# Four unrolled batches of a fallback path folded into two nested loops

## Chip, cores and metric

The kernel runs on one core of one Trainium2 chip. The metric is the time of one execution in microseconds (us), as a median of several runs. Work is spread over the core's engines: TensorE (PE, with its weight loads shown as PEld), VectorE (DVE), ScalarE (ACT), GpSimd (POOL), and SyncE (SP), which in this kernel issues most transfers. Each engine has a sequencer of its own that runs that engine's instruction stream in order. An instruction of the sequencer alone (a wait, a branch, a register load, the issue of a transfer) is written with a q: PEq, SPq.

## What is computed

```python
# q [4, 12288, 128], kv [4, 384, 32, 128], w_sr [128, 128]
kv_pool = kv.reshape(B, H // r, r, W // r, r, C).mean(axis=(2, 4))      # r = 4
k = v = kv_pool.reshape(B, -1, C) @ w_sr                                # 768 rows a batch
a = softmax(q @ k.T / sqrt(C));  x = (a @ v).reshape(B * 12288, C)
logits = x @ w_gate                                                     # 8 experts, the best 2
out = x + sum over the two experts of w * ((x @ A[e]) @ B[e])           # A: 128 to 16, B: 16 to 128
```

Spatial pooling and a projection give 768 keys a batch, which are the values as well; 49152 query rows attend to them, and each resulting row goes through the best two of eight rank-16 adapters.

## The kernel before, in words

The kernel has two paths in one program.

The **main path** (lines 51 to 605) does all of the work on ordinary data. It takes the 49152 rows in 96 chunks of 512. For each chunk it makes scores (L249) and their exponentials (L250), the weighted sum of the values (`weigh`, L260), normalises (L267, L271), transposes (L317), and runs the adapters (`down` L340, `apply_gate` L345, `up` L361, `give` L367 to L371, which also issues the transfer of the result). The order of all instructions is written out by hand (`manual_schedule`), with batch b+1's keys and values prepared while batch b is worked on. It works in 16-bit types and without the subtraction of the maximum, so it also counts, in `count_ok`, `values_ok`, `tail_ok` and `all_ok`, whether all sums and values lie in a safe range. The result is one integer, `bad`, written at L422.

The last two chunks are given out by ScalarE's queue (L603, L605, `give(..., queue=nc.scalar)`); all earlier results go through SP's queue.

The **general path** (lines 610 to 695) stands behind `tc.If(bad_v != 0)`. Every engine loads `bad` into a register (L607) and branches on it (L610). Where `bad` is zero, an engine jumps over the whole general path to a short block that stands behind it in its instruction stream. In that block each engine waits for its own last work and brings the semaphores to the values that the general path would have left; SP waits there for the transfers whose semaphores the general path uses, one semaphore after another (these waits carry the line of the If, L610). Then comes an end block, in which SP waits once more for every semaphore of the kernel, and all engines meet at a barrier twice (these carry the line of the call, L721).

Before the change the general path is, for each of four batches, written out four times: keys (L620 to L624) and values (L625 to L631) in float32 from the pooled rows `kpT[b]` in SBUF, then a hardware loop over 128 rows at a time (`tc.For_i`, L632) with a body of 20-odd operations.

Of the kernel before, what the change touches and what calls it, by code (L numbers as in the profile page):

```python
# [10 lines left out]
FP32 = mybir.dt.float32  # L11
# [10 lines left out]
def kernel(  # L22
# [10 lines left out]
    nc = tc.nc  # L33
    P = 128
    B, N, C = q.tensor.shape
# [3 lines left out]
    NKV = (H // 4) * (W // 4)  # L39
# [12 lines left out]
    kvpool = ctx.enter_context(tc.tile_pool(name="kvpool", bufs=4))  # L52
# [12 lines left out]
    qdram = ctx.enter_context(tc.tile_pool(name="qdram", bufs=1, space=bass.MemoryType.DRAM))  # L65

    def mtile(shape, dtype=FP32, name="hd"):
        return ps_h.tile(shape, dtype, tag="hd", name=name)

    mm = nc.tensor.matmul  # L70
# [7 lines left out]
    kvt = {}  # L78
# [38 lines left out]
    w_sr_sb = const.tile([P, P], FP32)  # L117
# [3 lines left out]
    wext = const.tile([P, C + E], FP32)  # L121
# [11 lines left out]
    kpT, kfT, vext = {}, {}, {}  # L133
# [363 lines left out]
    for c in range(1, NCH - 1):  # L497
        b, k = divmod(c, CPB)
# [11 lines left out]
        if cs < NCH and cs % GRP == 0:  # L510
            g = cs // GRP
# [98 lines left out]
    with tc.If(bad_v != 0):  # L610
# [5 lines left out]
        big2 = kvpool.tile([P, 4 * 1024], FP32, tag="kvt", name="g_e")  # L616
        e = big2[:, 0:NKV]
        eT = big2[:, 1024:1024 + NKV].rearrange("p (j t) -> p j t", j=NJ)
        for b in range(B):
            for h in range(2):  # L620
                s = slice(h * NKV // 2, (h + 1) * NKV // 2)
                k_ps = mtile([P, NKV // 2], name="gk_ps")
                mm(k_ps, w_sr_sb, kpT[b][:, s], start=True, stop=True)
                nc.vector.tensor_copy(k32[:, s], k_ps)  # L624
            for h in range(2):  # L625
                v_ps = mtile([P, NJ // 2, C + E], name="gv_ps")
                for g in range(NJ // 2):
                    j = h * NJ // 2 + g
                    mm(v_ps[:, g], kpT[b][:, j * P:(j + 1) * P], wext,
                       start=(g == 0), stop=(g == NJ // 2 - 1))  # L630
                nc.vector.tensor_copy(v32[:, h * NJ // 2:(h + 1) * NJ // 2], v_ps)  # L631
            with tc.For_i(b * N, (b + 1) * N, P) as t0:  # L632
                qt = run.tile([P, C], FP32, tag="g_q", name="g_q", bufs=1)
                nc.sync.dma_start(qt, qflat[bass.ds(t0, P), :])
                q_ps = mtile([P, P], name="gq_ps")
# [4 lines left out]
                for h in range(2):  # L640
                    mm(s_ps[:, h, 0:NKV // 2], qTf, k32[:, h * NKV // 2:(h + 1) * NKV // 2],
                       start=True, stop=True)
# [9 lines left out]
                for h in range(2):  # L652
                    e_ps = mtile([P, NJ // 2, P], name="ge_ps")
                    for g in range(NJ // 2):
                        j = h * NJ // 2 + g
                        mm(e_ps[:, g], e[:, j * P:(j + 1) * P], id_f32, is_transpose=True,
                           start=(g == 0), stop=(g == NJ // 2 - 1))
# [68 lines left out]
```

## Time and profile before

| what | us |
|---|---|
| median of 3 runs | 410.38 (409.85 to 410.66) |
| the profiled execution's own time | 410.03 |
| its span, from the first to the last instruction | 408.2 |
| around the span | 1.8 |
| PE busy | 385.4 (94% of the span) |
| DVE busy | 346.5 (85%) |
| ACT busy | 298.2 (73%) |
| POOL busy | 164.6 (40%) |

The granted TensorE clock is 0.993 on average. A row of the profile names the line, the engine, the operation, the tiles as out<-in, and the count. The queues of transfers are listed with packets, megabytes and the share of time; the kind `instruction` is the fetching of instructions from memory by the engines' sequencers.

### The profile page before, as it was taken

The page shows a single profiled execution, that of the slowest core. Times are in us where ns is not written, and L with a number is a line of the kernel's source. Part 1 is how long each engine was busy: PE and PEld are TensorE (multiplying, and loading weights), DVE is VectorE, ACT ScalarE, POOL GpSimd, SP SyncE. Part 2 cuts the span into 40 slices and gives each one's busy share as a digit, 9 for nine tenths or more (in the row PEclk, how much of TensorE's full clock was granted, in tenths as well). Part 3 has the DMA queues.
Part 4 walks back from the last instruction along what each step waited for, and adds up shares of the span by engine and source line. Part 5 has one row for each costly group of instructions (what it writes and reads, how often), then busy time and mean ns, then how long its engine had stood idle before and what let it go on. Part 6 is the DMA issues. An engine that isn't in the chain of part 4 may idle for free.

```text
span 408.2 us, 11562 instructions
## 1 busy us (share of the span) xinstructions
PE 385.4 (94%) x4607; PEld 306.0 (75%) x4607; DVE 346.5 (85%) x972; ACT 298.2 (73%) x357; POOL 164.6 (40%) x314
## 2 busy tenths in 40 slices
PE   4888999999999999999999999999999999999992
PEld 1446777887878787887878787777878788787792
DVE  3765799898899899898899899898899989899982
ACT  1648887886778877886678877876777888877751
POOL 1011489782113487882113487892212212122120
PEclk9999999999999999999999999999999999999997
DMA  8979899979467999979378999798185474221113
GB/s 256 404 234 174 260 292 231 303 164 156 117 119 127 327 244 284 318 175 157 92 143 133 323 219 296 241 260 161 54 181 117 142 159 130 79 79 68 66 75 140
DMA packets 69789, 76.52 MB, mean 187 GB/s; under 512 B 49664, under 2 KB 49920, under 8 KB 69376
## 3 DMA queue, kind: packets, MB, share of 16 engines
q1 hardware_dynamic: 67264, 63.45, 55.6%
q0 software_dynamic: 704, 11.54, 16.5%
q10 hardware_dynamic: 1760, 0.73, 0.7%
q8 instruction: 38, 0.62, 0.6%
q14 instruction: 23, 0.19, 0.1%
HBM read 50.53 MB, written 36.70 MB: 214 GB/s over the span
## 4 chain that ended last, share of the span: by engine, by line
PE 82%; DVE 10%; ACT 2%; issue 2%; DMA 2%; SPq 0%; DVEq 0%
PE xps L260 32%; PE sg L249 27%; PE t_ps L317 9%; PE d_ps L361 5%; PE h_ps L340 4%; DVE xn L271 2%; DVE hg L345 2%; DMA kvt<-in_kv_dram 2%; ACT tt L250 1%; PE v_ps L174 1%; DVE top L278 1%; PE k_ps L167 1%; DVE vmax L207 1%; DVE osb L369 1%; DVE xh L326 1%
## 5 line engine op out<-in xcount | busy, mean ns | idle before, releaser
L250 ACT ACTIVATE tt<-sg 128x1024 f16<-128x1024 f32 x288 | 282.8, 1022 | 76.7 <-PE sg L249 75.7
L249 PE MATMUL sg<-qT,kfT 128*128 128x512 bf16 x576 | 170.8, 379 | 1.5 <-ACT tt L250 0.7
L260 PE MATMUL xps<-vext,tt 128*128 128x137 f16 x2304 | 170.8, 224 | 0.5 <-DVE xn L271 0.4
L260 PEld LDWEIGHTS <-tt 128*128 128x128 f16 x2304 | 154.0, 112 | 23.1 <-DVE xn L271 1.5
L369 DVE TENSOR_TENSOR osb<-d_ps,xn 128x512 f32<-128x512 f32 x90 | 62.1, 690 | 17.3 <-PE d_ps L361 13.9
L271 DVE TENSOR_TENSOR xn<-xps,rinv_all 128x548 f32<-128x548 f32 x96 | 69.9, 729 | 3.3
L284 POOL TENSOR_TENSOR m<-top 128x8 f32<-128x8 f32 x47 | 10.9, 232 | 152.1 <-DVE top L278 151.9
L143 POOL TENSOR_TENSOR kvt<-kvt 128x1024 f32<-128x1024 f32 x27 | 64.0, 2370 | 3.9 <-DMA kvt<-in_kv_dram 1.5
L345 DVE TENSOR_TENSOR hg<-h_ps,gw 128x512 bf16<-128x512 f32 x94 | 63.8, 679 | 0.6 <-PE h_ps L340 0.4
L326 DVE COPY xh<-t_ps 128x1024 bf16<-128x1024 bf16 (+1 forms) x93 | 62.5, 672 | 0.0
L361 PEld LDWEIGHTS <-xh 128*128 128x128 bf16 x384 | 29.2, 98 | 26.1 <-issue 6.1
L249 PEld LDWEIGHTS <-kfT 128*128 128x128 bf16 x576 | 45.2, 98 | 3.7 <-issue 1.7
L340 PEld LDWEIGHTS <-xh 128*128 128x128 bf16 x384 | 29.2, 98 | 20.9 <-issue 0.7
L278 DVE MAX8 top<-xn 128x8 f32<-128x8 f32 x384 | 36.0, 156 | 3.3
L361 PE MATMUL d_ps<-b_bf,xh 128*128 128x128 bf16 x360 | 34.8, 219 | 3.3 <-DVE hg L345 3.0
L340 PE MATMUL h_ps<-a_bf,xh 128*128 128x128 bf16 x376 | 36.3, 219 | 0.6 <-DVE cnt L409 0.6
L317 PE MATMUL t_ps<-id_bf,xn 128*128 128x128 bf16 x376 | 36.3, 219 | 0.0
L317 PE MATMUL t_ps<-id_bf,hg 128*128 128x128 bf16 x376 | 36.3, 219 | 0.0
L299 POOL TENSOR_SCALAR th<-th 128x64 f32<-128x64 f32 x47 | 17.4, 370 | 37.4 <-ACT th L297 37.4
L317 PEld LDWEIGHTS <-xn 128*128 128x128 bf16 x384 | 26.0, 98 | 0.0
L317 PEld LDWEIGHTS <-hg 128*128 128x128 bf16 x384 | 25.4, 98 | 0.1
L267 DVE RECIPROCAL rinv_all<-xps 128x4 f32<-128x4 f32 x96 | 17.6, 183 | 8.2 <-PE xps L260 5.2
(103 smaller groups left out, 220.1 us busy)
## 6 DMA issues: line engine op xcount, KB each, us to landing
kvt<-in_kv_dram SPq DMA_DIRECT2D x48, 512.0 KB, 7.2
out_dram<-osb SPq DMA_DIRECT2D x94, 256.0 KB, 3.1
q_bf<-in_q_dram POOLq DMA_DIRECT2D x22, 512.0 KB, 6.6
q<-in_q_dram SPq DMA_DIRECT2D x2, 1024.0 KB, 10.1
out_dram<-osb ACTq DMA_DIRECT2D x2, 256.0 KB, 3.4
qT<-q_bf SPq DMA_TRANSPOSE x22, 7.1
w_in<-in_w_sr_dram ACTq DMA_DIRECT2D x1, 64.0 KB, 1.9
a_f<-in_moe_A_dram ACTq DMA_DIRECT2D x1, 64.0 KB, 10.1
```

Of the source, the lines that this page charges most:

```text
L143: eng.tensor_tensor(v[:, 0], v[:, 0], v[:, d], op=ALU.add)
L249: mm(sg[:, k], kfT[b][:, j * P:(j + 1) * P], qc, start=True, stop=True)
L250: nc.scalar.activation(tt[c][:, 2 * r:2 * r + 2], sg, AF.Exp, bias=0.0, scale=scale)
L260: mm(o, tt[c][:, j, rows], vext[b][:, j], start=(j == 0 and s % 2 == 0), stop=(j == NJ - 1 and s % 2 == 1), skip_group_check=True)
L271: nc.vector.tensor_tensor(xn[c].rearrange("p (b s) v -> p b s v", b=2), xv, ri.rearrange("p (b s) -> p b s", b=2).unsqueeze(3).broadcast_t ...
L278: nc.vector.max(gin[c // 2][:, (c % 2) * NS + s], xn[c][:, s, C:C + E])
L317: mm(t_ps[:, k, s], src, id_bf, is_transpose=True, start=(i == 0), stop=(i == len(todo) - 1), skip_group_check=True)
L326: nc.vector.tensor_copy(xh[:, lo:hi_], t_ps[:, lo:hi_])
L340: mm(hps[c][:, s], xT[c][:, s], a_bf, start=(s == 0), stop=(s == NS - 1))
L345: nc.vector.tensor_tensor(hg[c].rearrange("p s (e r) -> p (s e) r", r=RK), hps[c].rearrange("p s (e r) -> p (s e) r", r=RK), g.rearrange(" ...
L361: mm(dps[c][:, s], hgT[c][:, s], b_bf, start=(s == 0 and not plus_x), stop=(s == NS - 1), skip_group_check=True)
L369: nc.vector.tensor_tensor(osb, dps[c], xn[c][:, :, 0:C], op=ALU.add)
```

## The change

The four copies become one, inside a loop over the batches. A loop body can't choose among four SBUF tiles by a register, so the four pooled tiles are first written to a new DRAM tile `kp_all`, and each round of the outer loop reads one of them back into `kp`. The inner loop's offset is computed as `b * N + t`. All of it lies inside the If; lines 1 to 618 are as before. In the changed kernel, lines of the general path stand 5 or 6 further down, and the line of the call is L727.

```diff
         eT = big2[:, 1024:1024 + NKV].rearrange("p (j t) -> p j t", j=NJ)
+        kp_all = qdram.tile([B, P, NKV], FP32, name="kp_all")
         for b in range(B):
+            nc.sync.dma_start(kp_all[b], kpT[b])
+        kp = kvpool.tile([P, 4 * 1024], FP32, tag="kvt", name="g_kp")[:, 0:NKV]
+        with tc.For_i(0, B) as b:
+            nc.sync.dma_start(kp, kp_all[bass.ds(b, 1)].rearrange("o p k -> p (o k)"))
             for h in range(2):
                 s = slice(h * NKV // 2, (h + 1) * NKV // 2)
                 k_ps = mtile([P, NKV // 2], name="gk_ps")
-                mm(k_ps, w_sr_sb, kpT[b][:, s], start=True, stop=True)
+                mm(k_ps, w_sr_sb, kp[:, s], start=True, stop=True)
                 nc.vector.tensor_copy(k32[:, s], k_ps)
             for h in range(2):
                 v_ps = mtile([P, NJ // 2, C + E], name="gv_ps")
                 for g in range(NJ // 2):
                     j = h * NJ // 2 + g
-                    mm(v_ps[:, g], kpT[b][:, j * P:(j + 1) * P], wext,
+                    mm(v_ps[:, g], kp[:, j * P:(j + 1) * P], wext,
                        start=(g == 0), stop=(g == NJ // 2 - 1))
                 nc.vector.tensor_copy(v32[:, h * NJ // 2:(h + 1) * NJ // 2], v_ps)
-            with tc.For_i(b * N, (b + 1) * N, P) as t0:
+            with tc.For_i(0, N, P) as t:
+                t0 = b * N + t
                 qt = run.tile([P, C], FP32, tag="g_q", name="g_q", bufs=1)
```

In the built programs, which show the order of instructions and no time, every instruction ahead of the branch of L610 is the same on all five engines. Behind it, two things differ: the general path is shorter, and the block that is jumped to has one wait of SP fewer. Before, SP waits at L610 for the semaphores of eight transfer queues, DMAHW0 to DMAHW7 in this order; after, for seven, DMAHW3 being left out because the shorter path doesn't use it. DMAHW2 belongs to the transfer of L603 and DMAHW3 to that of L605. In the end block SP still waits for all eight, DMAHW3 in its eighth wait of twelve, PE's own semaphore in the eleventh and ACT's in the twelfth.

## The prediction

> **What bounds the kernel now.** I began with the page, to see which engine carries the time and whether the changed lines run at all.
>
> ```profile
> span 408.2 us, 11562 instructions
> ...
> PE 385.4 (94%) x4607; PEld 306.0 (75%) x4607; DVE 346.5 (85%) x972; ACT 298.2 (73%) x357; POOL 164.6 (40%) x314
> ...
> PE 82%; DVE 10%; ACT 2%; issue 2%; DMA 2%; SPq 0%; DVEq 0%
> ```
>
> TensorE is busy 94% of the span, and the chain of work is 82% PE. None of that work is edited: the edit lies wholly behind the branch of L610. No view has a row of L611 to L695, so the general path is jumped over, and only what the jump and the code behind it cost can change. So I read the chain in order of time, from 400 us on (start, duration, piece).
>
> ```profile
> 400.64 0.68 DVE osb L369
> 401.32 0.44 DVEq L607
> 401.76 0.15 DVE osb L369
> ```
>
> The last piece ends at 401.76 + 0.15 = 401.9. The span ends at 408.2. **6.3 us at the end hold no engine work**; there the sequencers branch and wait. The view of line L610 shows how (count, ns least/median/most, first and last start).
>
> ```profile
> L610 SPq EVENT_SEMAPHORE  x8: 17/17/17, 401.8 to 406.1; - x8
> L610 POOLq COMPARE_BRANCH  x1: 45/45/45, 401.0 to 401.0; - x1
> L610 SPq COMPARE_BRANCH  x1: 53/53/53, 401.3 to 401.3; - x1
> L610 PEldq COMPARE_BRANCH  x1: 4067/4067/4067, 401.7 to 401.7; - x1
> L610 DVEq COMPARE_BRANCH  x1: 72/72/72, 401.8 to 401.8; - x1
> ...
> L610 ACTq COMPARE_BRANCH  x1: 54/54/54, 403.3 to 403.3; - x1
> L610 ACTq EVENT_SEMAPHORE  x1: 17/17/17, 403.7 to 403.7; - x1
> L610 PEldq EVENT_SEMAPHORE  x1: 51/51/51, 405.8 to 405.8; - x1
> ```
>
> The same branch takes four engines 45 to 72 ns and PE 4067 ns. PE passes its wait at 405.8. SP's own eight waits last until 406.1. Two of them are long: the single starts in the narrow windows 403 to 405, 405.75 to 405.84 and 405.84 to 405.9, and the waits of SP's queue from 400 us on.
>
> ```profile
> L610 SPq EVENT_SEMAPHORE  x1: 17/17/17, 404.3 to 404.3; - x1
> L610 SPq EVENT_SEMAPHORE  x1: 17/17/17, 405.8 to 405.8; - x1
> L610 SPq EVENT_SEMAPHORE  x1: 17/17/17, 405.9 to 405.9; - x1
> ...
> SPq L610 <- SPq L610: 4.4, 4, 2.3
> ```
>
> Up to 404.3 (2.3 us) SP waits for DMAHW2, and up to 405.8 for DMAHW3: the landings of the last two results. These are the transfers that ACT issues at L371, one at 401.3 and one at 401.9; above them, for comparison, SP's last one, issued at 400.0 (each from the line's view in a window of its own, with its time to landing).
>
> ```profile
> L371 SPq DMA_DIRECT2D out_dram<-osb x1: 333/333/333, 400.0 to 400.0; - x1
> ...
> DMA to landing us min/median/max: 2.0/2.0/2.0
> ...
> L371 ACTq DMA_DIRECT2D out_dram<-osb x1: 362/362/362, 401.3 to 401.3; - x1
> ...
> DMA to landing us min/median/max: 3.0/3.0/3.0
> ...
> L371 ACTq DMA_DIRECT2D out_dram<-osb x1: 350/350/350, 401.9 to 401.9; - x1
> ...
> DMA to landing us min/median/max: 3.8/3.8/3.8
> ```
>
> 401.3 + 3.0 = 404.3 and 401.9 + 3.8 = 405.7: SP's two stops. Equal transfers of 256 KB, 2.0 against 3.0 and 3.8. What else the transfer engines carry then, from the queues in the window 402 to 405, below the same two queues from 0 to 400:
>
> ```profile
> q14 instruction: 4, 0.03, 4.6%
> q8 instruction: 1, 0.02, 2.1%
> ...
> q8 instruction: 36, 0.59, 0.6%
> q14 instruction: 18, 0.15, 0.1%
> ```
>
> In 3 us there are five instruction fetches, against 54 in the 400 us before. So the end is: five branches, five fetches on the same transfer engines as the last two results, results late, SP late, and PE late for itself at the same 405.8.
>
> **The change, part by part.**
>
> *Ahead of the branch*: no instruction is added, removed or moved on any engine; cost 0. The new DRAM tile stands behind the old one, and the old one keeps its place; cost 0.
>
> *PE's branch.* q8 moved 0.59 MB in 36 fetches, 16.4 KB each, while PE did 4566 matmuls and 4567 loads (row below): 9133 / 36 = 254 instructions a fetch, so about 64 bytes each and 256 to a page, one fetch whenever PE enters a page. From 397.0 on:
>
> ```profile
> 397.00:402.00 5.00, 3.87 (x43) 3.16 (x42) 2.95 (x8) 2.13 (x4) 0.00 (x0) 1.00 0.57 213
> 0.00:397.00 397.00, 381.50 (x4566) 302.86 (x4567) 343.51 (x965) 296.05 (x354) 164.57 (x314) 1.00 0.75 189
> ...
> q8 instruction: 1, 0.02, 40.7%
> ...
> L358 PE MATMUL e<-xn,id_f x24: 274/275/328, 393.6 to 398.9; 128*128 128x128 f32 x24
> ...
> L184 PE MATMUL kp_ps<-id_f,kvt x6: 272/273/336, 13.0 to 26.6; 128*128 128x128 f32 x6
> ```
>
> The third row is the window 396.9 to 397.1: the last fetch before the branch. 43 + 42 = 85 PE instructions follow, so the branch stands some 85 into a page, whose successor has just been fetched. How far it jumps: a float32 matmul counts twice (L358, 24 for 12 calls), a transpose once (L184, 6 for 6), each with a load. A batch of the general path has 8 matmuls ahead of its loop and 10 with 9 transposes in it: 18 x 4 + 9 x 2 = 90 instructions, about 27 more for loop control in the built program; four batches are some 470. 85 + 470 = 555 is past 512, in the page after the next: not fetched, hence the 4.07 us. Afterwards one batch with two loops' control is some 145: 85 + 145 = 230, the page PE is in. I expect **PE's branch at 0.05 to 0.07 us**, as on the other four, and its fetch gone. By itself this saves nothing, since SP is held to 405.8 by a result.
>
> [...]
>
> *The other fetches.* By the same count in pages of 0.15 MB / 18 = 8.3 KB or 128 instructions, ACT's jump falls from about 116 to 55 instructions, DVE's from 197 to 76, POOL's from 104 to 52, SP's from 151 to 86. None of the four stalled. I expect about half of the five fetches to go, and those of PE and ACT surely.
>
> *SP's waits.* Of the first group DMAHW3 is gone. After DMAHW2 SP goes straight on, as it now does after DMAHW3: from 405.8 to 408.2, **2.4 us** (405.9 to 406.1 three more waits, then the end block). DMAHW3 comes up again as the eighth wait of the end block, PE's in the eleventh (starts from the end block in narrow windows: 406.4 to 406.56, 406.95 to 407.02, 407.2 to 407.26):
>
> ```profile
> L721 SPq EVENT_SEMAPHORE  x1: 28/28/28, 406.5 to 406.5; - x1
> L721 SPq EVENT_SEMAPHORE  x2: 28/28/28, 406.9 to 407.0; - x2
> L721 SPq EVENT_SEMAPHORE  x1: 28/28/28, 407.2 to 407.2; - x1
> ```
>
> So the end comes at the latest of three: DMAHW2's landing + 2.4; DMAHW3's + 408.2 - 407.0 = 1.2; PE's or ACT's wait + 408.2 - 407.2 = 1.0.
>
> *Sum.* DMAHW2's transfer takes between 2.0 (SP's last, undisturbed) and 3.0 (as now). With about half of the fetches gone I take the middle, 2.5: landing 401.3 + 2.5 = 403.8, end **406.2**. DMAHW3 would have to land after 405.0 to matter, over 3.1 against 3.8 now; with two fewer fetches I expect 2.5 to 3.0. PE passes by 402.5, ACT at 403.7 + 1.0 = 404.7: neither matters. The gain is 408.2 - 406.2 = 2.0 us; by the ends 2.0 and 3.0 it is 2.5 and 1.5. On the profiled execution's 410.03 that is 408.0. It lay 0.35 below the median of 410.38, which gives 408.4; I write **408.3**.
>
> **Rivals.**
>
> 1. *PE's stall stays* (any taken branch of PE flushes what it holds, or its distance has nothing to do with it). For: PE is the only engine that stalled, and it had instructions queued. Against: the count of 555 against 512. Then PE passes at 405.8 and its fetch still disturbs the second result, landing 405.8. Ends: DMAHW2 404.3 + 2.4 = 406.7, DMAHW3 405.8 + 1.2 = 407.0, PE 405.8 + 1.0 = 406.8. The end is 407.0, a gain of 1.2: 408.8 to 409.2. The lost wait alone brings it.
> 2. *Nothing that can be measured.* The general path doesn't run, and the end hangs on when a result lands. If the first of the two took 3.7, near the 3.8 of the second now, DMAHW2 would land at 401.3 + 3.7 = 405.0, the end would be 405.0 + 2.4 = 407.4, and the gain 0.8 or less: 409.6 to 410.6. For: equal transfers spread from 2.0 to 3.8 here, so landings are not steady. Against: that spread stands beside five fetches in 3 us.
> 3. *Slower: the miss moves to ACT.* The end blocks shift against the pages on all engines. If ACT's target falls on a page that it doesn't hold, its branch at 403.3, the last of all, takes PE's 4.07 us, and with a transfer engine still busy some 5: its wait moves from 403.7 to 408.7, the end to 408.7 + 1.0 = 409.7, 1.5 later: 411.9. It decides from a miss of over 4.3 us (403.7 + 4.3 + 1.0 = 409.0, 0.8 over 408.2). Against: the jump becomes shorter, and a longer one was held.
>
> **How the numbers follow.** A measurement of this kernel can tell about 0.2%, here 0.8 us. Forecast 0.70 (407.5 to 409.0), stall stays 0.12, nothing 0.12, slower 0.04, and 0.02 for a faster end than 407.5. The range 407.5 to 409.6 takes in the forecast with both its bounds and the first rival, and leaves out most of the other two. Faster: 0.70 + 0.02 + 0.11 = 0.83; same: 0.12 + 0.01 = 0.13; slower 0.04.
>
> **What would show it.** In the changed profile: PE's COMPARE_BRANCH of L610 under 0.1 us; q8 with 36 or 37 fetches, not 38, and q14 under 23; seven SP waits at L610, the third passed near 403.8; the first ACT transfer at L371 landing in 2.3 to 2.8 us; the end 2.4 us after it, span near 406.2, and all up to 401.9 as before. The forecast is wrong if PE's branch still takes 4 us, if the two landings stay at 3.0 and 3.8 with the fetches gone, or if another engine shows a long branch.

## The result: 405.51 us against 409.9, of which the change itself holds about 1.6 to 1.8

In the first comparison the changed kernel took 405.51 us (median of 5 runs, 405.44 to 407.24), the kernel before 409.9 (5 runs, 409.46 to 410.66). The ratio is 0.9928, with a 95% interval of 0.99 to 0.9957. The forecast was 408.3 with a range of 407.5 to 409.6: the right direction, and too small a step by far.

The profile of the changed kernel, first the page: span and engines, then the two queues of instruction fetches.

```profile
span 403.5 us, 11488 instructions
...
PE 381.3 (95%) x4534; PEld 306.2 (76%) x4607; DVE 344.2 (85%) x972; ACT 297.7 (74%) x357; POOL 164.2 (41%) x314
...
q8 instruction: 36, 0.59, 0.6%
q14 instruction: 20, 0.16, 0.1%
```

The span is 4.7 shorter, and 2 + 3 fetches are gone. (73 matmul records are missing here, 4534 of 4607; the weight loads are complete.) The last pieces of the chain from 397.8 us on show where the engines' work ends:

```profile
398.64 0.44 DVEq L607
399.07 0.15 DVE osb L369
```

At 399.07 + 0.15 = 399.2, where before had 401.9. So the 4.7 us fall into two parts, which I call by these names from here on: **the first part**, up to the end of the last L369, 401.9 before and 399.2 now, 2.7 less; and **the tail** behind it, 408.2 - 401.9 = 6.3 before and 403.5 - 399.2 = 4.3 now, 2.0 less. The prediction was about the tail alone. The tail's rows, line L610 of the changed kernel:

```profile
L610 SPq EVENT_SEMAPHORE  x7: 17/17/17, 399.2 to 401.8; - x7
L610 POOLq COMPARE_BRANCH  x1: 45/45/45, 398.3 to 398.3; - x1
L610 SPq COMPARE_BRANCH  x1: 53/53/53, 398.6 to 398.6; - x1
L610 PEldq COMPARE_BRANCH  x1: 228/228/228, 399.0 to 399.0; - x1
L610 DVEq COMPARE_BRANCH  x1: 72/72/72, 399.1 to 399.1; - x1
L610 PEldq EVENT_SEMAPHORE  x1: 51/51/51, 399.2 to 399.2; - x1
...
L610 ACTq COMPARE_BRANCH  x1: 54/54/54, 400.6 to 400.6; - x1
```

PE's branch fell from 4067 to 228 ns, the other four are unchanged, and SP has seven waits. The last two results, each in a window of its own, and the queues in the window 399 to 402:

```profile
L371 ACTq DMA_DIRECT2D out_dram<-osb x1: 362/362/362, 398.7 to 398.7; - x1
...
DMA to landing us min/median/max: 2.8/2.8/2.8
...
L371 ACTq DMA_DIRECT2D out_dram<-osb x1: 350/350/350, 399.3 to 399.3; - x1
...
DMA to landing us min/median/max: 2.8/2.8/2.8
...
q10 hardware_dynamic: 288, 0.52, 46.7%
q14 instruction: 1, 0.01, 0.6%
```

They land after 2.8 and 2.8 in place of 3.0 and 3.8, beside one fetch in place of five. SP's third wait, single in the window 401.49 to 401.55, and the first of the end block:

```profile
L610 SPq EVENT_SEMAPHORE  x1: 17/17/17, 401.5 to 401.5; - x1
...
L727 SPq EVENT_SEMAPHORE  x1: 28/28/28, 401.9 to 401.9; - x1
```

SP stops for DMAHW2 until 401.5 (398.7 + 2.8), and the end comes 403.5 - 401.5 = 2.0 later.

### The profile page after: what moved, and what is told of

The parts are those of the page before. It is cut to its first block, busy times and chain, and to the rows that moved or that the text cites. A ratio compares the mean times of both kernels' runs of the same rounds, so it can differ in the third digit from the quotient of the medians.

```text
span 403.5 us, 11488 instructions
## 1 busy us (share of the span) xinstructions
PE 381.3 (95%) x4534; PEld 306.2 (76%) x4607; DVE 344.2 (85%) x972; ACT 297.7 (74%) x357; POOL 164.2 (41%) x314
## 4 chain that ended last, share of the span: by engine, by line
PE 85%; DVE 8%; issue 2%; ACT 2%; DMA 1%; DVEq 0%; ACTq 0%
PE xps L260 33%; PE sg L249 24%; PE t_ps L317 9%; PE d_ps L361 6%; PE h_ps L340 5%; PE w_ps L448 2%; DVE xn L271 2%; DVE hg L345 2%; ACT tt L250 1%; PE v_ps L174 1%; DMA w_gate_sb<-in_moe_w_gate_dram 1%; PE k_ps L167 1%; DVE vmax L207 1%; DVE osb L369 1%; DVE xh L326 1%
## 5 line engine op out<-in xcount | busy, mean ns | idle before, releaser
L249 PE MATMUL sg<-qT,kfT 128*128 128x512 bf16 x503 | 155.2, 379 | 1.7 <-ACT tt L250 0.7
L369 DVE TENSOR_TENSOR osb<-d_ps,xn 128x512 f32<-128x512 f32 x90 | 62.1, 690 | 17.6 <-PE d_ps L361 13.8
L345 DVE TENSOR_TENSOR hg<-h_ps,gw 128x512 bf16<-128x512 f32 x94 | 63.8, 679 | 0.6 <-PE h_ps L340 0.4
L143 POOL TENSOR_TENSOR kvt<-kvt 128x1024 f32<-128x1024 f32 x27 | 63.9, 2366 | 0.9 <-DMA kvt<-in_kv_dram 0.2
L361 PEld LDWEIGHTS <-xh 128*128 128x128 bf16 x384 | 29.3, 98 | 24.1 <-issue 3.7
L361 PE MATMUL d_ps<-b_bf,xh 128*128 128x128 bf16 x360 | 34.8, 219 | 3.3 <-DVE hg L345 1.7
L299 POOL TENSOR_SCALAR th<-th 128x64 f32<-128x64 f32 x47 | 17.3, 368 | 37.5 <-ACT th L297 37.5
```

The source lines that it names most:

```text
L143: eng.tensor_tensor(v[:, 0], v[:, 0], v[:, d], op=ALU.add)
L249: mm(sg[:, k], kfT[b][:, j * P:(j + 1) * P], qc, start=True, stop=True)
L345: nc.vector.tensor_tensor(hg[c].rearrange("p s (e r) -> p (s e) r", r=RK), hps[c].rearrange("p s (e r) -> p (s e) r", r=RK), g.rearrange(" ...
L361: mm(dps[c][:, s], hgT[c][:, s], b_bf, start=(s == 0 and not plus_x), stop=(s == NS - 1), skip_group_check=True)
L369: nc.vector.tensor_tensor(osb, dps[c], xn[c][:, :, 0:C], op=ALU.add)
```

## The experiments

**Theory A**: the change works in the tail alone, as predicted; the 2.7 us of the first part are the spread of single executions. **Theory B**: the change moves the first part too, by its DRAM tile (memory laid out otherwise) or by the program's length. Rival 1 of the prediction (PE's stall stays whatever the distance) is tried along with them. In each experiment's profile I take the first part and the tail apart as above. "PE's jump" is the number of PE's instructions between the branch and its target in the built program, and "two results land after" is the time from issue to landing of the last two. "Beside" gives the kernel before, timed on the same chip in the same job.

| kernel | PE's jump | first part | tail | two results land after | median | beside | ratio (95%) |
|---|---|---|---|---|---|---|---|
| before | 470 | 401.9 | 6.3 | 3.0, 3.8 | | | |
| changed | 145 | 399.2 | 4.3 | 2.8, 2.8 | 405.51 | 409.9 | 0.9928 (0.99 to 0.9957) |
| e1 before again | 470 | 401.8 | 6.7 | 3.0, 4.3 | 408.71 | 408.7 | 1.0001 (0.9978 to 1.0025) |
| e2 DRAM tile only | 470 | 402.5 | 6.3 | 3.0, 3.8 | 409.35 | 408.7 | 1.0005 (0.9984 to 1.0026) |
| e3 short, no DRAM tile | 145 | 403.6 | 4.0 | 2.8, 2.8 | 406.71 | 408.7 | 0.9967 (0.9946 to 0.9987) |
| e4 PE's jump long | 475 | 400.6 | 5.2 | 2.9, 3.9 | 407.47 | 408.7 | 0.9976 (0.9958 to 0.9993) |
| e5 changed again | 145 | 401.2 | 4.3 | 2.9, 2.8 | 407.17 | 408.9 | 0.9946 (0.9918 to 0.9975) |
| e6 wait back | 145 | 400.8 | 4.8 | 2.8, 2.8 | 407.57 | 408.9 | 0.9956 (0.9926 to 0.9986) |
| e7 SP's page moved | 145 | 402.1 | 3.5 | 2.1, 2.2 | 406.1 | 408.9 | 0.9927 (0.9899 to 0.9954) |
| e8 sums later | 145 | 399.2 | 4.4 | 2.9, 2.8 | 406.11 | 408.9 | 0.9928 (0.9902 to 0.9954) |
| e9 before, sums later | 470 | 399.4 | 6.3 | 3.0, 3.9 | 407.63 | 408.68 | 0.9975 (0.9958 to 0.9992) |
| e10 sums later again | 145 | 400.7 | 4.4 | 3.0, 3.0 | 406.03 | 408.68 | 0.9925 (0.99 to 0.995) |
| e11 both | 145 | 400.5 | 3.5 | 2.1, 2.2 | 405.04 | 408.68 | 0.99 (0.9873 to 0.9928) |
| e12 changed a third time | 145 | 400.3 | 4.2 | 2.8, 2.8 | 407.71 | 408.67 | 0.9972 (0.9943 to 1.0001) |

The two columns of parts already answer most: **the tail follows the program to 0.4 us, the first part doesn't follow its length at all.** A profile is of one execution, often not the one in the middle: e10's took 407.15, the longest of its runs, and e11's 406.0, the longest too.

### e1: the kernel before, a second time

Only a comment differs.

> The kernel before, unchanged but for a comment, for a second profile of it. Split: from the start to the end of the last L369 (401.9 in the first profile, 399.2 in the changed kernel's), and from there to the end (6.3 against 4.3). Theory A, the 2.7 us ahead of the branch are luck of landings in one execution: this profile's first part can fall anywhere from 399 to 402, and the time spreads by as much. Theory B, they belong to the program (its length or its DRAM tile changes how transfers meet): the first part is 401.5 to 402.3 again, the time 409.5 to 410.7. By both the tail is 6.0 to 6.5 with PE's branch at 3.5 to 4.5 us.

First part 401.8, tail 6.7, PE's branch 4407 ns. The first part alone can't decide between A and B, but the times speak for A's spread: the same kernel, 35 times on one chip, ran from 407.58 to 411.22. Three runs of 409.85 to 410.66, on which the prediction's range was built, show a quarter of that spread.

### e2: the DRAM tile alone

```diff
+        kp_all = qdram.tile([B, P, NKV], FP32, name="kp_all")
+        for b in range(B):
+            nc.sync.dma_start(kp_all[b], kpT[b])
         for b in range(B):
             for h in range(2):
```

> Four unrolled batches as before, plus the DRAM tile and its four writes in the general path, which is not run. Only memory is laid out otherwise. Theory B by the DRAM tile: the first part falls to about 399.2 and the time to about 407.7, the tail stays at 6.3. Theory B by program length, and theory A: time as before, 409.5 to 410.7, first part as in the repeated kernel before.

First part 402.5, tail 6.3, ratio 1.0005. Memory laid out otherwise is worth nothing that can be measured. Theory B by the DRAM tile falls.

### e3: the short program without the DRAM tile

The keys of batch 0 stand for all four batches in the general path, which is not run.

```diff
-        kp_all = qdram.tile([B, P, NKV], FP32, name="kp_all")
-        for b in range(B):
-            nc.sync.dma_start(kp_all[b], kpT[b])
-        kp = kvpool.tile([P, 4 * 1024], FP32, tag="kvt", name="g_kp")[:, 0:NKV]
+        kp = kpT[0]
         with tc.For_i(0, B) as b:
-            nc.sync.dma_start(kp, kp_all[bass.ds(b, 1)].rearrange("o p k -> p (o k)"))
```

> Two nested loops as in the changed kernel, but no DRAM tile: the keys of batch 0 serve for all four batches in the general path, which is not run. PE's jump is 145 instructions; SP waits at L610 for DMAHW4 and DMAHW5 alone. The tail is DMAHW3's landing + 1.2 or DMAHW2's + 1.3: with landings of 2.8 us as in the changed kernel 3.5 to 4.0 us, shorter than its 4.3. Theory B by program length: first part about 399.2, time 404.7 to 405.5. Theory B by the DRAM tile: first part about 401.9, time 407.3 to 408. Theory A: anything between.

First part 403.6, the longest of all fourteen profiles, under the short program, and a median of 406.71 where theory B by the length asked for 404.7 to 405.5: it falls too. The tail is 4.0, at the upper end of what was expected.

### e4: PE's jump made long again

```diff
+    PAD = 165
...
+        pad = mtile([P, P], name="pad")
+        for i in range(PAD):
+            mm(pad, id_bf, id_bf, start=(i == 0), stop=(i == PAD - 1))
         kp_all = qdram.tile([B, P, NKV], FP32, name="kp_all")
```

> The changed kernel with 165 dead bf16 matmuls in the general path, so that PE alone jumps 475 instructions again (475 against 145), while the other four engines and SP's waits are the changed kernel's. Page theory: PE's branch takes 3.5 to 4.5 us again, one PE fetch stands in the tail, PE's wait passes 4.1 us after its branch started and the end comes 1.0 after it or 1.2 after DMAHW3's landing: tail 4.8 to 5.3 against 4.3, time about 0.5 to 1.0 over the changed kernel's. If distance has nothing to do with it, the branch stays at 0.2 and the time is the changed kernel's.

Lines stand one further down here. PE's branch, and the fetches from 401 to 405.5:

```profile
L611 SPq COMPARE_BRANCH  x1: 53/53/53, 400.0 to 400.0; - x1
L611 PEldq COMPARE_BRANCH  x1: 4127/4127/4127, 400.3 to 400.3; - x1
...
L611 PEldq EVENT_SEMAPHORE  x1: 51/51/51, 404.5 to 404.5; - x1
...
q8 instruction: 2, 0.03, 3.4%
q14 instruction: 1, 0.01, 0.4%
```

475 instructions take 4127 ns, 145 take 228: **the distance decides**, and rival 1's cause falls. Where between 145 and 470 the border lies, and whether it is the end of a page, was not tried. With PE's fetches back (q8: two in this window) the second result lands after 3.9 again, and SP, which no longer waits for it at L610, waits for it in the end block: 400.6 + 3.9 + 1.2 = 405.7, the span's 405.8. The tail of 5.2 is close to what rival 1's sum (a gain of 1.2, so 5.1) gives for a stall that stays.

### e5 and e12: the changed kernel again

Only a comment differs.

> The changed kernel, unchanged but for a comment, timed on the same chip as the other three and profiled a second time. Theory A (only the tail belongs to the change, the first part is landing luck): tail 4.2 to 4.4 again, first part anywhere from 399 to 404, and over many runs the time is 1.7 to 2.5 us below the kernel before, not 4.4. Theory B (the change moves the first part too): first part 399.2 again and 4 us below.

> The changed kernel a third time, for the size of the change alone. Tail 4.2 to 4.4 and 2.0 around the span, against 6.3 and 1.8: by theory A the median lies 1.5 to 2.3 us under the kernel before; by theory B about 4.4 under it, as in the first comparison.

Tails 4.3 and 4.2; first parts 401.2 and 400.3, not 399.2. The medians lie 1.7 and 1.0 under the kernel before, not 4.4. e12's 1.0 is under the 1.5 that theory A gave for it; its interval of 0.9943 to 1.0001 is wide and reaches past 1, so that no difference lies within it, and its 12 runs reach from 405.78 to 410.7. The sizes are those of theory A or a little less; the 4.4 that theory B asks for is outside both intervals.

### e6: the eighth wait put back

```diff
                 nc.sync.dma_start(out[bass.ds(t0, P), :], og)
+                nc.sync.dma_start(q_bf[0:P], id_bf)
```

> The changed kernel with one more transfer of SP in the loop body of the general path, which is not run, so that SP waits at L610 for all eight queues again; the jumps stay short (PE 145, SP 91). Then the end hangs on DMAHW3's landing in place of DMAHW2's: 0.5 us later in the changed kernel's profile. Tail 4.7 to 4.9 against 4.26. If the order of the waits were worth what rival 1 gave it, 1.2 us, the tail would be 5.5; if nothing, 4.26.

The dead transfer uses a fourth queue in the loop, so SP waits for all eight at L610:

```profile
L610 SPq EVENT_SEMAPHORE  x8: 17/17/17, 400.8 to 403.9; - x8
...
L371 ACTq DMA_DIRECT2D out_dram<-osb x1: 350/350/350, 400.9 to 400.9; - x1
...
DMA to landing us min/median/max: 2.8/2.8/2.8
```

SP now stops for the second result, 400.9 + 2.8 = 403.7, and the tail is 4.8: the order of the waits is worth 0.5 us in the short program. The shorter jumps are worth the rest, 6.3 - 4.8 = 1.5: 1.0 because the second result lands after 2.8 in place of 3.8, and some 0.4 because SP goes from its last wait at L610 to the end block at once (403.93 to 404.00 in the trace), where before had 0.4 in between. That the first of these is the fetches' doing, e4 and e7 show; what the 0.4 were was not tried.

### e7: SP's page moved

```diff
+        if c == 40:
+            for i in range(50):
+                nc.sync.drain()
```

> The changed kernel with 50 drains of SP in chunk 40 of the main path, which do nothing but move SP's instructions on, so that SP enters its next page before the branch and its fetch in the tail (0.3 us, at 400.3 in the changed kernel) goes. In the changed kernel 15 of the 16 parts of each of the last two transfers land 0.6 to 0.7 us ahead of the sixteenth. If the fetch on that transfer engine holds it up, both land at 2.1 to 2.2 us after the issue in place of 2.8, and the tail is 3.5 to 3.6 against 4.26. If the sixteenth is late for another reason, the tail stays at 4.2 to 4.3.

The queues of the changed kernel's tail had one fetch left. Here, from 402 to the end, there is none, and both results land sooner (windows of L371; the q10 row is that of the window 402 to 405.62):

```profile
q10 hardware_dynamic: 288, 0.52, 38.0%
...
L371 ACTq DMA_DIRECT2D out_dram<-osb x1: 362/362/362, 401.6 to 401.6; - x1
...
DMA to landing us min/median/max: 2.1/2.1/2.1
...
L371 ACTq DMA_DIRECT2D out_dram<-osb x1: 350/350/350, 402.2 to 402.2; - x1
...
DMA to landing us min/median/max: 2.2/2.2/2.2
```

The tail is 3.5. One fetch of 8 KB costs the two transfers 0.6 to 0.7 us, although they have 512 KB: in the changed kernel's trace 15 of the 16 parts of the first result have landed by 400.76 and the last at 401.49, and SP stops until that last one (401.5). In e7 all 16 lie within 0.2 us (403.45 to 403.63). That the late part shared a transfer engine with the fetch fits both, but was not shown: no view names the engine.

### e8 to e10: where the first part's spread comes from

Counting PE's weight loads in the traces, I compared the time between the same two instructions in seven profiles (before, changed, e1 to e5). Apart from the first 61 loads, four stretches of 100 loads hold nearly all differences: those at 1600, 1800, 2700 and 2900. From load 2900 to 3000, for example, it is 8.55 before, 8.05 changed, 9.89 in e3 and 9.03 in e5; from 3000 to 3600 it is 50.10 or 50.11 in all seven. The stretches lie where GpSimd's sums of the next batch's key rows (L143) come up. The rows of L143 on GpSimd's queue (ns least/median/most), in this order before, changed and e3:

```profile
L143 POOLq EVENT_SEMAPHORE  x21: 17/17/1162, 47.5 to 265.1; - x21
```

```profile
L143 POOLq EVENT_SEMAPHORE  x21: 17/17/43, 46.8 to 260.0; - x21
```

```profile
L143 POOLq EVENT_SEMAPHORE  x21: 17/17/2524, 47.9 to 266.1; - x21
```

The 1162 and 2524 ns end with the last part of a transfer of key rows, at 263.0 and 264.8 us. Waits that stand at the sum itself are not in this row, and e2's row reads 17/17/43 like the changed kernel's. They stand among GpSimd's waits (total, times, longest), here before, changed and e2:

```profile
POOL kvt L143 <- DMA kvt<-in_kv_dram: 1.5, 1, 1.5
```

```profile
POOL kvt L143 <- DMA kvt<-in_kv_dram: 0.2, 1, 0.2
```

```profile
POOL kvt L143 <- DMA kvt<-in_kv_dram: 4.1, 6, 1.2
```

GpSimd waits there for key rows that land late, for up to 2.5 us, and hardly at all in the changed kernel's first profile, the lucky one. Behind it in GpSimd's queue stand the gate weights (L299, L300), on which L345 on VectorE and then L361 on PE depend. The waits between those two, before and then e3 (total, times, longest):

```profile
PE d_ps L361 <- DVE hg L345: 3.0, 7, 1.0
```

```profile
PE d_ps L361 <- DVE hg L345: 4.4, 6, 1.7
```

So I moved the sums and all that follows them by two chunks, in the changed kernel (e8, e10) and in the kernel before (e9):

```diff
-        if k in (5, 9, 13):
+        if k in (7, 11, 15):
...
-        elif k in (7, 11, 15):
+        elif k in (9, 13, 17):
...
-        if k == 17:
+        if k == 19:
             pooled_transposed(b)
...
```

> The changed kernel with GpSimd's sums of the key rows two chunks later (chunks 7 to 17 of a batch in place of 5 to 15), and what follows them too. In six profiles the first part differs only at the start and at four places where GpSimd waits at L143 for a late kvt transfer and holds up the gate weights behind it, 0.3 to 2 us each. If that is the cause of the spread, these places go: first part 397.5 to 400, the time 1 to 2.5 us under the changed kernel on the same chip, with a smaller spread. If the cause lies elsewhere, nothing changes or the later sums cost time elsewhere.

> The kernel before with the sums two chunks later: a quieter first part under the unrolled general path. The difference between this and the next kernel is the change itself with the spread of the first part taken away. Theory A: tail 6.2 to 6.8, median 1.8 to 2.5 us above the next kernel's. Theory B, by which the change moves the first part too: more than 3.5 us above.

> The changed kernel with the sums two chunks later, on the same chip as the one before. Tail 4.2 to 4.4, no wait of over 0.3 us at the four places of L361, first part 399 to 400.5, median 405.8 to 406.5.

The four places are quiet in all three: in none does GpSimd wait at L143 for a transfer, and PE's waits for L345 are the same (e8's row):

```profile
PE d_ps L361 <- DVE hg L345: 1.5, 4, 0.6
```

The spread shrinks: e9's 12 runs lie from 407.33 to 408.45, while the kernel before ran from 407.4 to 410.49 beside it. e8's lie from 405.51 to 408.13, one of 413.61 apart, and its median is 1.1 under that of e5 on the same chip. What is left of the spread stands at the start: e10's first part of 400.7 is 1.3 above e9's, and the loads 40 to 61 take 4.95 in e9 and 6.43 us in e10. With the first part this quiet, e9 and e10 measure the change alone: 407.63 - 406.03 = **1.6 us**, a little under the 1.8 to 2.5 that theory A gave and far from theory B's 3.5 or more. The runs of the two don't overlap (407.33 and above, 407.15 and below).

### e11: both additions, for the fastest version

e8's and e7's edits together.

> The changed kernel with the sums two chunks later and SP's 50 drains: both gains together, if they are independent. Tail 3.5, first part 399 to 400.5, median 405.0 to 405.8, about 0.7 us under the second kernel and 3 to 3.6 us under the kernel before. If the drains shift SP's page fetches into a worse place of the main path, the first part rises by up to 1 us and the gain is under 0.3 us.

405.04 (404.83 to 406.0), 0.99 of the kernel before (0.9873 to 0.9928), 1.0 under e10; tail 3.5. Its median is the lowest here. The late landings are not all gone: in its profile GpSimd waits 1.2 us for a transfer of key rows that lands at 179.7, and the loads 1900 to 2000 take 8.89 us in place of 7.77.

## Why the prediction was right in its mechanism and wrong in its range

*What bounds the end* was right: branches, fetches and the last two landings, with no engine work. *PE's branch* was right in kind, by distance (e4: 4127 ns over 475 instructions, against 228 over 145), and at 0.23 us in place of 0.05 to 0.07 too low in size, without consequence. The count behind it, 256 to a page and 555 past 512, was an estimate from 36 fetches for 9133 instructions, and its border was not tried. What the runs show is one fetch of PE inside the long branch of before (q8 at 403.3) and none beside the short one (no q8 from 399 to 402 in the changed kernel). *SP's waits* were right: DMAHW2's landing sets the end (401.5 + 2.0 = 403.5).

*The sum* gave the tail a gain of 2.0, and it measured 2.0. But that was two errors that cancelled. I had DMAHW2's landing at 2.5 and it took 2.8, because I took a middle between two ends; the one fetch that is left still holds up one of sixteen parts by as much as 0.7 (e7), so "half of the fetches gone" doesn't give half of the delay. And I had 2.4 from that wait to the end, and it is 2.0: before, 0.4 lay between the waits of L610 (until 406.1) and the end block (from 406.5), and now 401.8 is followed by 401.9. I had carried the 2.4 over unexamined. *The other fetches*: I expected about half of five to go, and four went.

*Ahead of the branch, cost 0* is the step that failed, not in its cause but in what it was taken for. The instructions there are the same, and by e2, e3, e5 and e12 the change moves nothing there. But cost 0 was carried into the sum as if the first part would end at 401.9 again, and it ended at 399.2, 2.7 us sooner. The same instructions don't take the same time: the first part lies between 399.2 and 403.6 in fourteen profiles, by landings of key rows at four places (e8 to e10), and at the start, where the cause was not tried. The range took in the bounds of the tail's landings and the three runs shown, and had no term for this. Such a term could have been read from the profile of before: PE's 3.0 us of waiting for L345, GpSimd's waits at L143 for transfers that land after 7.2 us in the median. With 2 us to either side the range would have been 406.3 to 410.3, and 405.51 would still lie outside it. The base was high too: 410.03 and 410.38 were taken for the kernel's time, and its 104 later runs, on other chips, have a median of 408.7. From there a gain of 1.8 leads to 406.9, also below the range.

*The time around the span* was taken as unchanged. It was 1.8 before (410.03 - 408.2) and is 2.0 now (405.51 - 403.5), and 1.8 and 2.0 are also the means over the 35 runs of before and the 12 of e5. This takes 0.2 back: 2.0 - 0.2 = 1.8 is the change's gain by the profiles, 1.6 by e9 and e10, 1.7 and 1.0 by the medians of e5 and e12. In the profile a fetch that stood in the tail before, at 407.2, now comes 1.6 us behind the span's end; that this is the cause was not tried.

*The rivals*: rival 1's cause falls by e4, and its sum is e4's tail. Rival 2 falls: the fetches were what held the landings up (e4 for the second result, 3.9 against 2.8; e7 for what was left, 2.1 and 2.2 against 2.8). Rival 3 didn't occur; ACT's branch is 54 ns before and after.

**Open**: why in the first comparison all five runs of before lay at 409.46 or above and four of five of the changed kernel at 405.82 or below. On the other chips the kernel before took 407.25 to 413.43 in 104 runs, 34 of them at 409.46 or above; the changed kernel took 405.78 to 410.7 in 24 runs (e5 and e12), one of them at 405.82 or below, and three of its first five runs lie under all 24. So the 2.6 us by which the first comparison exceeds the change's own 1.8 lie in the first part (in the two profiles 0.7 us in the first 40 loads, and 0.4, 1.1 and 0.5 at the loads 1600, 2700 and 2900), at places where other profiles vary too, but why they all fell one way stays open. Whether the chip, or the place in memory where a program is loaded, sets the landings for a whole series was not tried.

## What to carry to other kernels

Code that is jumped over can still cost: here a jump of 470 instructions held PE for 4.1 us, and the fetches in the tail delayed the last results (before 3.0 and 3.8 us with five fetches beside them, the changed kernel 2.8 and 2.8 with one, e7 2.1 and 2.2 with none), which are what the end waits for. So count the distance of the jump on each engine, and the fetches in the last few us, before anything else in a tail. And a median of three runs that lie close together says little about the spread of landings; where an engine's queue waits for transfers, as GpSimd's does here for up to 2.5 us, put that spread into the range, or take it away first and measure then, as e9 and e10 do.

## What was not expected of the hardware

- With one 8 KB fetch of instructions beside them, the two 256 KB results landed 0.6 to 0.7 us later (2.8 in the changed kernel against 2.1 and 2.2 in e7), more than the fetch itself takes (0.3 us in the trace of the changed kernel).
- PE's branch over 145 instructions took 227 or 228 ns in all nine profiles of it, the other engines' branches 45 to 72; over 470 to 475 it took 4067 to 4407 ns in five.
- A long stretch of the main path repeated to 0.01 us between executions (50.10 or 50.11 us for the 600 weight loads from 3000 on, in seven profiles), and nearly all of the first part's spread sits at four places and at the start.
